# Seven loads of v on ScalarE's queue, and three large products of zeros in place of 48 small ones

## The chip, the cores and the metric

The kernel runs on one core of a Trainium2 chip. The metric is the device time of one execution in microseconds; less is better. The kernel before takes 585.13 us (median of 3 runs, 584.51 to 585.97).

## What is computed

Three stages follow one another. Block retention (a linear attention with decay) over `q`, `k`, `v` of shape (2, 8, 768, 64) in float32, in blocks of 64 positions:

```python
for b in range(nb):
    intra = np.einsum('bhic,bhjc->bhij', qb, kb) * Dmask[None]
    intra = np.einsum('bhij,bhjd->bhid', intra, vb)
    inter = np.einsum('bhid,bhde->bhie', qb * lam_pow[None], kv_state)
    out[:, :, sl] = intra + inter
    kv_state = lam_block[None, :, None, None] * kv_state + np.einsum('bhsd,bhse->bhde', kb * rev_pow[None], vb)
```

Its output, as 1536 rows of 512, goes through two feed-forward stages with hidden width 2048: `h = x @ w_in`, a pointwise function (mish in the first, elu in the second), `g @ w_out`. The weights come as 64-bit floats and are turned into pairs of 32-bit parts on the core.

## The kernel before

Retention goes in chunks of 128 positions: `chunks` has twelve, numbered from 0, the two batches in turn; a chunk holds all 8 heads. The loop `for n in range(NC + 2)` (L368 to L393) is a software pipeline written out by hand. In turn n it issues the loads of k and q of chunk n+3 and of v of chunk n+1 (L369, L370), then weights (`LOAD`, L371), then does: the late part of chunk n-2's output (`second_part`: `xl`, `sd`), scores and decay of chunk n (`sc`, `am`), the transposes of chunk n+1 (`Tp` in PSUM, copied to `T` by ScalarE, L237), `scaled_q` of chunk n+1 (tile `q`), `block_state` (`sbd`, ScalarE, L350), the output products of chunk n-1 (`o`, L305, and the state product `st`, L314) and their copy `xh` (ScalarE, L325). GpSimd makes `kd` and scales `sd`. All these steps are pinned: each engine takes its own in program order.

All loads but the small one of `lam` stand in SyncE's (SP) queue, so the order of their issue is that of L369 to L371 over the turns. Every load of k, q or v brings 256 KB in runs of 256 B (64 floats); tiles `kn`, `qn`, `vn` have four buffers each, so v of chunk n+1 takes the buffer of chunk n-3. A block of weights (`raw`) brings 512 KB, for `w_in` in runs of 1 KB. Weights of the first group are loaded at turns 5 and 8 to 13, and VectorE turns them into pairs beside the chunks (`w_steps`, L86; `STEPS`, L548). After the last scores come two units of the first feed-forward product (`EARLY`), then the rest of it on TensorE.

Before the loop, TensorE is given products of zeros (`idle`): `warm(7)` (seven calls of 128 x 128 by 128 x 128 in float32, two instructions each), then the transposes of chunk 0 in two parts with `warm(2)` between them, then `warm_tiles(24)`: 24 calls with 64 x 64 operands in the four quarters of the array, 48 instructions. `warm(2)` stands once more in turn 0. Nothing reads the results.

Of the kernel before, what the change touches and what calls it, by code (L numbers as in the profile page):

```python
# [8 lines left out]
F32 = mybir.dt.float32  # L9
# [9 lines left out]
def kernel(  # L19
# [12 lines left out]
    nc = tc.nc  # L32
    P = 128
    B, H, S, D = q.shape
# [3 lines left out]
    PR = H // 2  # L38
# [87 lines left out]
    def retention(beside_load, beside_step, at_end):  # L126
# [6 lines left out]
        psO = es.enter_context(tc.tile_pool(name="psO", bufs=1, space=PSUM))  # L133

        chunks = [(b, c) for c in range(NCH) for b in range(B)]
        NC = len(chunks)
        nat, tr, sc, am, q2s, kds, done = {}, {}, {}, {}, {}, {}, {}

        def pin(ins):
            tc.keep_in_program_order(ins)  # L140
            return ins

        def load(n, names, parts=1):
            if not 0 <= n < NC:
                return
            b, c = chunks[n]
            for nm in names:
                nat[n, nm] = io.tile([P, H, D], F32, tag=nm + "n", name=nm + "n")
            for y in range(parts):
                for nm in names:  # L150
                    src, t = {"k": k, "q": q, "v": v}[nm], nat[n, nm]
                    hs = slice(y * H // parts, (y + 1) * H // parts)
                    pin(nc.sync.dma_start(  # L153
                        out=t[:, hs],
                        in_=src[b, hs, c * P:(c + 1) * P, :].rearrange("h p d -> p h d"),
                    ))
# [3 lines left out]
        nc.scalar.dma_start(out=lam_b.rearrange("p h o -> p (h o)"), in_=lam.partition_broadcast(P))  # L160
        load(1, "kq")
        load(2, "kq")
        load(0, "v")

        idle = cst.tile([P, P], F32, name="idle")
# [46 lines left out]
        def warm(count):  # L212
            ps = psO.tile([P, PR, P], F32, tag="o", name="warm")
            for _ in range(count):
                pin(nc.tensor.matmul(ps[:, 0], lhsT=idle, rhs=idle, start=True, stop=True))

        def transposes(n, parts=1):

            T2 = P // 2
            both = wk.tile([P, 2, PR, P], F32, tag="T", name="T")  # L220
            ps = psT.tile([P, 2, 2, PR, T2], F32, tag="T", name="Tp")
            for y in range(parts):
                if y > 0:
                    warm(2)
                rs = slice(y * PR // parts, (y + 1) * PR // parts)
                for z, nm in enumerate(("k", "q")):
                    x = nat[n, nm]
                    for r in range(rs.start, rs.stop):
                        for h in range(2):
                            rows = slice(h * T2, (h + 1) * T2)  # L230
                            pin(nc.tensor.transpose(  # L231
                                ps[:, h, z, r],
                                x[rows, 2 * r:2 * r + 2].rearrange("p h d -> p (h d)"),
                                ident[rows, rows],
                            ))
                if parts == 1:
                    pin(nc.scalar.activation(  # L237
                        out=both.rearrange("p z r (h t) -> p h (z r) t", h=2),
                        in_=ps.rearrange("p h z r t -> p h (z r) t"), func=AF.Copy,
                    ))  # L240
                else:
                    for z in range(2):
                        pin(nc.scalar.activation(
                            out=both[:, z, rs].rearrange("p r (h t) -> p h r t", h=2),
                            in_=ps[:, :, z, rs], func=AF.Copy,
                        ))
            tr[n] = both[:, 0], both[:, 1], ps

        def scaled_k(n):
            if n >= NC:  # L250
                return
            kd = None
            if chunks[n][1] < NCH - 1:
                kd = wk.tile([P, H, D], F32, tag="kd", name="kd", bufs=3)
                pin(nc.gpsimd.tensor_tensor(
                    out=kd, in0=nat[n, "k"], in1=dm[:, :, P - 1:P].to_broadcast([P, H, D]), op=ALU.mult
                ))
            kds[n] = kd

        def scaled_q(n):  # L260
            if n < NC and chunks[n][1] > 0:
                q2 = wk.tile([P, PR, P], F32, tag="q2", name="q2", bufs=3)
                pin(nc.vector.tensor_tensor(  # L263
                    out=q2.rearrange("p r (h t) -> p h r t", h=2), in0=tr[n][2][:, :, 1],
                    in1=lq.rearrange("p r (h t) -> p h r t", h=2), op=ALU.mult,
                ))
                q2s[n] = q2

        def scores(n):
            kT, qT, _ = tr[n]  # L270
            ps = psS.tile([P, 2, PR, P], F32, tag="sc", name="sc")
            for r in range(PR):
                for hh in range(2):
                    rows = slice(hh * D, (hh + 1) * D)
                    last = pin(nc.tensor.matmul(  # L275
                        ps[:, hh, r], lhsT=kT[rows, r], rhs=qT[rows, r], start=True, stop=True
                    ))
            sc[n] = ps
            return last

        def decay(n):
            a = wk.tile([P, 2, PR, P], F32, tag="am", name="am")
            pin(nc.vector.tensor_tensor(
                out=a, in0=sc.pop(n), in1=dm.rearrange("p (r t) i -> p t r i", t=2), op=ALU.mult
            ))
            am[n] = a
# [34 lines left out]
        def first_part(n):  # L321
            o, st = done[n]
            b, c = chunks[n]
            t, col = divmod(n * P, TB)
            pin(nc.scalar.activation(out=xh[t][:, :, col:col + P], in_=o, func=AF.Copy))  # L325
            if st is not None and c > 0:
                pin(nc.gpsimd.tensor_tensor(out=sd[b], in0=sd[b], in1=lc, op=ALU.mult))

        def second_part(n):
            o, st = done[n]  # L330
            b, c = chunks[n]
            t, col = divmod(n * P, TB)
            pin(nc.vector.tensor_tensor(  # L333
                out=xl[t][:, :, col:col + P],
                in0=o,
                in1=xh[t][:, :, col:col + P].bitcast(F32),
                op=ALU.subtract,
            ))
            if st is not None:
                if c > 0:  # L340
                    pin(nc.vector.tensor_tensor(out=sd[b], in0=sd[b], in1=st, op=ALU.add))
                else:
                    pin(nc.vector.tensor_copy(sd[b], st))
# [7 lines left out]
                        out=sbd[b][rows, :, rows], in_=sd[b][rows], func=AF.Copy  # L351
                    ))


        def warm_tiles(count):

            ps = [psO.tile([P, PR, x], F32, tag=t, name="warm") for t, x in (("o", P), ("st", D))]
            for x in range(count):
                y, z = divmod(x % 4, 2)
                rows, cols = slice(y * D, (y + 1) * D), slice(z * D, (z + 1) * D)  # L360
                pin(nc.tensor.matmul(
                    ps[y][cols, 0, 0:D], lhsT=idle[rows, 0:D], rhs=idle[rows, 0:D], start=True, stop=True
                ))

        warm(7)
        transposes(0, 2)
        warm_tiles(24)
        for n in range(NC + 2):  # L368
            load(n + 3, "kq")  # L369
            load(n + 1, "v")  # L370
            beside_load(n, pin)  # L371
            if n >= 2:
                second_part(n - 2)
                beside_step(n, 0, pin)
            if n < NC:
                last = scores(n)
                decay(n)
            if n == 1:
                powers(8, P)
            if n + 1 < NC:  # L380
                transposes(n + 1)
            if n == 0:
                warm(2)
                scaled_k(0)
            if n + 1 < NC:
                scaled_q(n + 1)
            if n >= 2:
                block_state(n - 2)
            if 0 < n <= NC:
                outputs(n - 1)  # L390
                first_part(n - 1)
            scaled_k(n + 1)
            beside_step(n, 1, pin)  # L393
        with tc.issue_after(last.ins):
# [161 lines left out]
    def beside_load(n, pin):  # L556
        for m in LOAD.get(n, ()):
            pin(w_load(m))

    def beside_step(n, place, pin):  # L560
        for _ in range(STEPS.get((n, place), 0)):
            pin(next(todo))
# [6 lines left out]
    def first_units():  # L569
        for _ in todo:  # L570
            pass
        for u in range(EARLY):
            unit(u)
            weights_at(u)

    retention(beside_load, beside_step, first_units)
    open_late()
    for u in range(EARLY):
# [36 lines left out]
```

## Time and profile before

| | us |
|---|---|
| median of 3 runs | 585.13 (584.51 to 585.97) |
| the profiled execution | 584.7 |
| span of its instructions | 582.4 |
| PE busy | 574.4 (99%) |
| DVE busy | 430.9 (74%) |
| ACT busy | 231.5 (40%) |
| POOL busy | 18.9 (3%) |

PE is TensorE, PEld its weight loads, DVE VectorE, ACT ScalarE, POOL GpSimd; SPq is SyncE's queue. The span runs from the first to the last instruction of the program; the time of the execution has 2.3 us more around it. Busy time is an average over stages: retention takes about the first 60 us, the two feed-forward stages the rest.

### The profile page before, as it was taken

To read this page: it belongs to the slowest core of one execution; us is meant where nothing else is said; L and a number is where in the kernel's file an instruction comes from. 1 tells how busy PE (TensorE), PEld (TensorE's weight loads), DVE (VectorE), ACT (ScalarE), POOL (GpSimd) and SP (SyncE) were. 2 spreads that over 40 slices of the span, in tenths; PEclk is the share of its full clock that TensorE was granted. 3 is DMA by queue.
4 is the path that set the end of the run, shared out by engine and by line. 5 is a ranking of instruction groups with operands and counts; after the bars stand their busy time and mean duration, and the time that the engine had idled before them with its cause. 6 is when DMAs were issued, how large, how long until landed. Compare 5 with 4: busy or idle time off the path is not lost.

```text
span 582.4 us, 8221 instructions
## 1 busy us (share of the span) xinstructions
PE 574.4 (99%) x3282; PEld 481.2 (83%) x3282; DVE 430.9 (74%) x798; ACT 231.5 (40%) x390; POOL 18.9 (3%) x28
## 2 busy tenths in 40 slices
PE   7999999999999999999999999999999999999997
PEld 6988888888888888888888888888888888888886
DVE  5769999998399726993599956995499957944342
ACT  3655554344134124233346445555145235235220
POOL 4430000000000000000000000000000000000000
PEclk9999999999999999999999999999999999999999
DMA  9998333334023301322022221321022310000112
GB/s 172 214 219 233 109 110 108 110 111 142 0 74 108 109 1 37 106 79 69 1 72 73 73 73 36 110 74 71 1 73 72 109 36 1 1 1 0 73 54 92
DMA packets 61030, 46.67 MB, mean 80 GB/s; under 512 B 38848, under 2 KB 55488, under 8 KB 60992
## 3 DMA queue, kind: packets, MB, share of 16 engines
q1 hardware_dynamic: 60848, 46.14, 28.2%
q8 instruction: 26, 0.43, 0.3%
q14 instruction: 12, 0.10, 0.1%
q10 hardware_dynamic: 144, 0.00, 0.0%
HBM read 43.00 MB, written 3.15 MB: 79 GB/s over the span
## 4 chain that ended last, share of the span: by engine, by line
PE 93%; DMA 2%; DVE 2%; SPq 1%; ACT 1%; issue 1%; ACTq 0%
PE h L423 44%; PE y L465 43%; PE o L305 2%; PE y L480 2%; DMA qn<-in_q_dram 1%; DMA vn<-in_v_dram 1%; SPq L153 1%; PE sc L275 1%; PE Tp L231 1%; PE st L314 0%; DVE xl L333 0%; DVE b L104 0%; DVE u L111 0%; DVE q L263 0%; ACT xh L325 0%
## 5 line engine op out<-in xcount | busy, mean ns | idle before, releaser
L423 PE MATMUL h<-xh,w 128*128 128x512 f32 x768 | 240.7, 389 | 0.1
L423 PEld LDWEIGHTS h<-xh,w 128*128 128x128 f32 x768 | 144.1, 188 | 30.5 <-ACT w L118 0.6
L423 PE MATMUL h<-xl,w 128*128 128x512 f32 x384 | 149.4, 389 | 0.0
L465 PE MATMUL y<-w,g 128*128 128x512 f32 (+1 forms) x588 | 132.5, 385 | 0.0
L465 PEld LDWEIGHTS y<-w,g 128*128 128x128 f32 x588 | 108.9, 188 | 22.1
L465 PE MATMUL y<-g,w 128*128 128x512 f32 x528 | 121.5, 389 | 0.0
L465 PEld LDWEIGHTS y<-g,w 128*128 128x128 f32 x528 | 99.1, 188 | 20.6
L493 DVE TENSOR_TENSOR acc<-acc,y 128x512 f32<-128x512 f32 (+1 forms) x73 | 49.4, 677 | 58.6 <-PE y L465 58.6
L433 DVE TENSOR_TENSOR g<-g,g 128x512 fp32r<-128x512 f32 x96 | 65.9, 687 | 30.0 <-ACT g L432 27.5
L423 PEld LDWEIGHTS h<-xl,w 128*128 128x128 f32 x384 | 72.1, 188 | 14.9
L118 ACT ACTIVATE w<-m 128x512 fp32r<-128x512 f32 x64 | 40.2, 628 | 102.0 <-PE h L423 55.2
L432 ACT ACTIVATE g<-g 128x512 fp32r<-128x512 f32 x96 | 60.2, 628 | 16.3 <-DVE g L450 14.8
L119 DVE TENSOR_TENSOR w<-m,w 128x512 fp32r<-128x512 f32 x64 | 43.9, 686 | 24.4 <-ACT w L118 23.7
L441 ACT ACTIVATE g<-h 128x512 f32<-128x512 f32 x48 | 28.5, 596 | 71.1 <-PE h L423 71.1
L447 ACT ACTIVATE e<-h 128x512 f32<-128x512 f32 x48 | 28.6, 596 | 59.0 <-PE h L423 58.0
L450 DVE SCALAR_TENSOR_TENSOR g<-e,h 128x512 f32<-128x512 f32 x48 | 32.8, 683 | 17.1 <-ACT e L448 17.0
L104 DVE SCALAR_TENSOR_TENSOR b<-raw,b 128x512 int32<-128x512 int32 x64 | 44.1, 690 | 0.4
L111 DVE SCALAR_TENSOR_TENSOR u<-raw,u 128x512 f32<-128x512 uint32 x64 | 43.7, 684 | 0.2
L116 DVE TENSOR_TENSOR m<-b,u 128x512 f32<-128x512 f32 x64 | 43.7, 684 | 0.1
L448 ACT ACTIVATE e<-e 128x512 f32<-128x512 f32 x48 | 30.3, 631 | 1.1
L98 DVE TENSOR_SCALAR m<-m 128x512 f32<-128x512 f32 x64 | 27.1, 424 | 0.1
L107 DVE TENSOR_SCALAR u<-b 128x512 int32<-128x512 int32 x64 | 26.8, 420 | 0.4
(52 smaller groups left out, 304.3 us busy)
## 6 DMA issues: line engine op xcount, KB each, us to landing
raw<-in_moe_w_in_dram SPq DMA_DIRECT2D x32, 512.0 KB, 3.7
raw<-in_moe_w_out_dram SPq DMA_DIRECT2D x32, 512.0 KB, 3.3
vn<-in_v_dram SPq DMA_DIRECT2D x12, 256.0 KB, 5.2
kn<-in_k_dram SPq DMA_DIRECT2D x11, 256.0 KB, 5.2
qn<-in_q_dram SPq DMA_DIRECT2D x11, 256.0 KB, 5.0
out_dram<-acc SPq DMA_DIRECT2D x11, 256.0 KB, 2.0
kn<-in_k_dram SPq DMA_DIRECT2D x2, 128.0 KB, 3.5
qn<-in_q_dram SPq DMA_DIRECT2D x2, 128.0 KB, 3.6
```

The lines of the kernel that those rows point to most:

```text
L104: yield nc.vector.scalar_tensor_tensor(out=b, in0=hw, scalar=-0x40000000, in1=b, op0=ALU.bitwise_and, op1=ALU.bitwise_or)
L111: yield nc.vector.scalar_tensor_tensor(out=uf, in0=lw, scalar=2.0 ** -52, in1=uf, op0=ALU.mult, op1=ALU.mult)
L116: yield nc.vector.tensor_tensor(out=mf, in0=bf, in1=uf, op=ALU.add)
L118: nc.scalar.activation(out=w[:, 0], in_=mf, func=AF.Copy)
L119: yield nc.vector.tensor_tensor(out=w[:, 1], in0=mf, in1=w[:, 0].bitcast(F32), op=ALU.subtract)
L423: nc.tensor.matmul(h, lhsT=lt, rhs=rt, start=(kk == 0 and n == 0), stop=(kk == KD - 1 and n == 2),)
L432: nc.scalar.activation(out=gg[:, 0], in_=g, func=AF.Copy)
L433: nc.vector.tensor_tensor(out=gg[:, 1], in0=g, in1=gg[:, 0].bitcast(F32), op=ALU.subtract)
L448: nc.scalar.activation(out=e, in_=e, func=AF.Exp, scale=-1.0)
L450: nc.vector.scalar_tensor_tensor(out=g, in0=e, scalar=-1.0, in1=h, op0=ALU.add, op1=ALU.max)
L465: nc.tensor.matmul(y, lhsT=lt, rhs=rt, start=(i == 0 and n == 0), stop=(i == G - 1 and n == 2),)
L493: nc.vector.tensor_tensor(out=dst, in0=dst, in1=y, op=ALU.add)
```

## The change

Two edits. First, `load` takes the queue that issues as a parameter. For n below `OTHER` = 4 the load of v of chunk n+1 stays where it was; from n = 4 on, that is for chunks 5 to 11 (the sixth and later, seven loads), it is issued by ScalarE, in program order behind `first_part(n - 1)`, whose instruction on ScalarE is `xh` of chunk n-1 (the first part of x). On ScalarE the next pinned instruction behind it is the copy `T` of the next turn. Second, `warm_tiles` goes, and `warm(3)` stands in place of `warm_tiles(24)`: three calls with full 128 x 128 operands, writing tile `o` only.

```diff
+        OTHER = 4
-        def load(n, names, parts=1):
+        def load(n, names, parts=1, queue=nc.sync):
...
-                    pin(nc.sync.dma_start(
+                    pin(queue.dma_start(
...
-        def warm_tiles(count):
-
-            ps = [psO.tile([P, PR, x], F32, tag=t, name="warm") for t, x in (("o", P), ("st", D))]
-            for x in range(count):
-                y, z = divmod(x % 4, 2)
-                rows, cols = slice(y * D, (y + 1) * D), slice(z * D, (z + 1) * D)
-                pin(nc.tensor.matmul(
-                    ps[y][cols, 0, 0:D], lhsT=idle[rows, 0:D], rhs=idle[rows, 0:D], start=True, stop=True
-                ))
-
         warm(7)
         transposes(0, 2)
-        warm_tiles(24)
+        warm(3)
         for n in range(NC + 2):
             load(n + 3, "kq")
-            load(n + 1, "v")
+            if n < OTHER:
+                load(n + 1, "v")
...
             if 0 < n <= NC:
                 outputs(n - 1)
                 first_part(n - 1)
+            if n >= OTHER:
+                load(n + 1, "v", queue=nc.scalar)
             scaled_k(n + 1)
```

## Rows read from the trace of the kernel before

**Rows 1.** Page, the span in 40 slices: busy tenths of PE, granted TensorE clock.

```profile
PE   7999999999999999999999999999999999999997
PEclk9999999999999999999999999999999999999999
```

**Rows 2.** Chain of waits in order of time: start us, us, what.

```profile
6.75 6.17 DMA vn<-in_v_dram
...
33.52 6.58 DMA qn<-in_q_dram
...
61.93 24.77 PE h L423 x108
```

**Rows 3.** Busy time in windows: the first line names the columns.

```profile
core 0: us, PE busy (x) PEld busy (x) DVE busy (x) ACT busy (x) POOL busy (x), PEclk, DMA share, GB/s
28.00:32.00 4.00, 4.00 (x86) 3.86 (x84) 2.90 (x5) 2.50 (x5) 1.64 (x2) 1.00 1.15 233
...
35.00:36.00 1.00, 1.00 (x26) 0.93 (x24) 1.00 (x2) 0.47 (x1) 0.18 (x1) 1.00 1.08 353
...
56.00:60.00 4.00, 4.00 (x22) 3.04 (x22) 4.00 (x11) 0.67 (x2) 0.00 (x0) 1.00 0.05 19
```

**Rows 4.** Timeline, 29.5 to 36.3 us: start, us, engine, line, tiles [idle before <-releaser].

```profile
29.54 0.60 ACT L325 ACTIVATE xh<-o 128x512 fp32r<-128x512 f32 x1
...
31.56 1.02 ACT L237 ACTIVATE T<-Tp 128x1024 f32<-128x1024 f32 x1 [1.42 <-PE Tp L231]
...
33.49 0.60 ACT L325 ACTIVATE xh<-o 128x512 fp32r<-128x512 f32 x1
...
34.12 0.69 DVE L333 TENSOR_TENSOR xl<-o,xh 128x512 fp32r<-128x512 f32 x1 [0.81 <-ACT xh L325]
...
35.05 1.22 DVE L283 TENSOR_TENSOR am<-sc,dm 128x1024 f32<-128x1024 f32 x1
...
36.28 1.04 PE L305 MATMUL o<-am,vn 128*64 128x128 f32 x16
```

**Rows 5.** Timeline, TensorE at chunk 9's transposes and at chunk 10's output.

```profile
40.14 0.47 PE L231 MATMUL Tp<-ident,qn 64*128 64x64 f32 x8 [1.02 <-DMA qn<-in_q_dram]
...
53.11 1.04 PE L305 MATMUL o<-am,vn 128*64 128x128 f32 x16
```

**Rows 6.** Timeline, issues in SyncE's queue, 33 to 48 us.

```profile
33.52 0.89 SPq L153 DMA_DIRECT2D qn<-in_q_dram  x1
34.50 2.33 SPq L153 DMA_DIRECT2D vn<-in_v_dram  x1
...
46.13 0.47 SPq L153 DMA_DIRECT2D vn<-in_v_dram  x1
46.65 1.08 SPq L75 DMA_DIRECT2D raw<-in_moe_w_in_dram  x1
```

**Rows 7.** Time to landing: all loads of v; on the page, loads of 128 KB.

```profile
DMA to landing us min/median/max: 4.4/5.2/8.0
...
kn<-in_k_dram SPq DMA_DIRECT2D x2, 128.0 KB, 3.5
```

**Rows 8.** Timeline, 5 to 14 us: the products of zeros and what follows them.

```profile
5.08 0.52 PEld L215 LDWEIGHTS warm<-idle 128*128 128x128 f32 x4
5.08 0.71 PE L215 MATMUL warm<-idle 128*128 128x128 f32 x4
...
6.30 0.93 PE L361 MATMUL warm<-idle 64*64 64x64 f32 x48
...
6.41 0.66 ACT L243 ACTIVATE T<-Tp 128x256 f32<-128x256 f32 x2 [0.56 <-PE Tp L231]
...
13.06 1.09 PE L305 MATMUL o<-am,vn 128*64 128x128 f32 x16 [1.46 <-DMA vn<-in_v_dram]
```

**Rows 9.** Instructions and their fetches: page, then transfers in 9.5:10 and 36.6:37 us.

```profile
PE 574.4 (99%) x3282; PEld 481.2 (83%) x3282; DVE 430.9 (74%) x798; ACT 231.5 (40%) x390; POOL 18.9 (3%) x28
...
q8 instruction: 26, 0.43, 0.3%
...
q8 instruction: 1, 0.02, 16.4%
...
q8 instruction: 1, 0.02, 19.8%
```

## The prediction

> **What bounds the kernel now.** I read the page's slices first. TensorE (PE) is 90% busy or more in all slices but the first and the last, at granted clock 0.9 to 1.0 throughout [rows 1]; so the time can change only where PE is not yet full. The chain of waits says where that ends: it goes through v of chunk 0 (6.75 to 12.92 us), later through q of chunk 9 (33.52 to 40.10 us), and from 61.93 us on PE runs without a gap to the last store [rows 2]. All of the change lies ahead of 61.93 us; what follows is a fixed 520.5 us (582.4 less 61.93). The sum is therefore: by how much does the point at 61.93 us move?
>
> Three limits lie close together there. **Loads:** while chunks stream, the DMA engines move 233 GB/s; a 256 KB load of k, q or v costs 262,144 B / 233 GB/s = 1.13 us, three per chunk 3.4 us. Weights, in longer packets, go at 353 GB/s, 524,288 B / 353 = 1.49 us each [rows 3]. **PE:** one chunk costs 3.95 us (`xh` of chunk 4 starts at 29.54, of chunk 5 at 33.49 us) [rows 4], and the one place where it stops late in the stage is 1.02 us for q of chunk 9 [rows 5]. **VectorE (DVE):** busy 4.00 of 4 us from 56 to 60 us, where before it was busy 2.90 [rows 3]: late in the stage the weight steps fill it, so a delay met there goes to the end in full.
>
> **Removed from SP, added to ScalarE (ACT).** Seven loads, v of chunks 5 to 11, leave SP's queue. On SP, k and q of the following chunks and the weights move up by one place for each v. The sequencer time that this frees (0.47 to 2.33 us per issue [rows 6]) buys nothing by itself: the loads move at the data rate [rows 3], and SP is ahead of them by the 5.2 us from issue to landing [rows 7]. I count 0 for it; the bytes to be moved before 61.93 us are the same.
>
> On ACT each issue stands behind `xh` of chunk n-1. ACT is then idle until the transposes are copied: 1.42 us between `xh` (ends 30.14) and `T` at 31.56 us [rows 4], and since a sequencer can go on to an issue while its engine works, the 0.60 us of `xh` may cover it too: 2.02 us at best, 1.42 at worst. Behind the issue are queued `T`, the two `sbd` copies and the next `xh`; for `xh` waits DVE (`xl` 0.81 us idle for it), behind that `am`, which ends at 36.27 us, and PE wants it at 36.28 [rows 4]. So this chain has no slack: what an issue takes beyond its cover is lost one to one. The trace has no 256 KB issue on ACT; the bounds are SP's shortest and longest, 0.47 and 2.33 us [rows 6]. ACT's queue has no backlog of its own, so I take the short one: 0 us, with 7 x (2.33 - 2.02) = 2.2 us as the upper bound. The slot's last readers are the products of chunk n-3, two turns of the loop earlier, so the added wait for them ends before it is reached: 0.
>
> **Order of landing.** This is the main term. Now SP issues in the order in which PE needs the data: k, then q of chunk 9 at 33.52 us, then v of chunk 7 at 34.50 us [rows 6]. Afterwards ACT issues v of chunk 7 as soon as `xh` of chunk 5 is under way (33.49 us [rows 4]), on a queue without the 5 us of backlog that SP's loads show (median 5.2 us to landing [rows 7]). PE wants that v in `outputs(7)`, after the transposes of chunk 9, whose q is already late [rows 5]. If the DMA engines serve both queues in turn, some of v's 1.13 us falls ahead of q. Bounds: 0 (SP's backlog goes first) and +1.13. q still has most of its 6.58 us [rows 2] before it when v starts, so I take nearly all, +1.0 us.
>
> The Trainium skill (DMA: Bandwidth & Descriptors, Queues, rings and completion order) says that an engine takes its queues in turn, packet by packet. No run here has yet shown two loaded queues; by that rule the term is +1.0, and by strict order of issue it is 0.
>
> **Three large products for 48 small ones.** On PE 48 small ones take 0.93 us from 6.30 us; four large ones take 0.71 us at a pace of 0.52/4 = 0.13, so six (three calls are six instructions, as 7 calls are 14) take 0.71 + 2 x 0.13 = 0.97 us [rows 8]. PE waits at their end for `T`, which ends at 7.07 us, either way, and at 13.06 us it still waits 1.46 us for v of chunk 0 [rows 8]: 0 us, cover 1.46 us. I take the granted clock to stay: the large products keep at least as much of the array busy. Were PE at 1.2 GHz afterwards, a chunk's 3.95 us of PE work would double, of which the stop hides 1.46: bound 0 to +2.5, taken 0.
>
> It has a side effect. PE gets 42 products and 42 weight loads fewer. The page counts 26 instruction fetches, 0.43 MB [rows 9], for 2 x 3282 PE instructions: 65 B each, a fetch of 16 KB per 252. With 84 fewer, each fetch comes a third of a period later, 84/170 of a chunk's instructions (86 and 84 in 4 us [rows 3]), some 2 us. Two fetches stand at 9.5 to 10 and 36.6 to 37 us [rows 9], right before the two loads that land late: v of chunk 0 takes 6.17 and q of chunk 9 6.58 us [rows 2] against the median of 5.2 [rows 7], 1.0 and 1.4 us more. Moved to about 38.7 us, the later fetch comes too late to hold up q. Bounds 0 and -1.4; I take -0.8, since the fetch may hold up k and q of chunk 10 instead. The 1.0 us at chunk 0 brings PE ahead, but q of chunk 9 is the later limit: 0 there.
>
> **The last v's.** SP, without v, issues the weights of the first group earlier, in one backlog, while v of chunk 10, until now issued at 46.13 us ahead of weights (46.65 us [rows 6]), comes from ACT behind `xh` of chunk 8, some 46.6 us. With a turn each, 1,024 packets of v meet 1,024 packets of weights (two loads of 512 packets): 1.13 + 2 x 1.49 = 4.1 us. A load of 128 KB with nothing ahead lands in 3.5 us, 2.9 without its data [rows 7]: 46.6 + 2.9 + 4.1 = 53.6 us, and PE wants it at 53.11 [rows 5]. Bounds 0 and +1.1 (a delay carried over); taken +0.4. The weights that come earlier gain nothing, since DVE is busy with older work.
>
> **Sum:** 0 + 0 + 1.0 - 0.8 + 0 + 0.4 = +0.6 us. The profiled execution took 584.7 us (span 582.4, 2.3 around it), so it would be 585.3; the median of the runs shown is 585.13, 0.4 above, and I forecast 585.7 us.
>
> **Rivals.**
> Faster: v does not get ahead of q, because SP's backlog is served first, and the moved fetch takes the whole 1.02 us stop away [rows 5]; with PE also ahead by what it gains at chunk 0, at most 1.0 + 1.0. For: loads, PE and DVE are within 0.5 us per chunk, so a small relief counts. Against: the bytes are the same, so a v that gives way to q is itself late. Time: 585.1 - 1.0 = 584.1, at most 583.1. Chance 0.22.
>
> Slower: ACT is held at its issue. If ACT's issue has to wait until the one that SP is at is through, it takes: up to 2.33 + 0.47 - 2.02 = 0.8 us each time, for PE through `T`, `xh`, `xl`, `am` [rows 4]. It decides from the point where wait and issue together pass 2.02 us. Three of seven issues that meet one of SP's as long as the 2.33 us [rows 6] cost 2.4, with the sum +3.0: 588.1 us. Against it: SP has fewer issues left to meet. Chance 0.20.
>
> The Trainium skill (Perfetto Trace Analysis, DMA Instruction — HWDGE (DVE, Sync)) tells of one descriptor block that an issuer locks; no row here shows such a wait.
>
> Nothing happens: v lands early, q at the same time, 585.1 us. Chance 0.13. My forecast: 0.45.
>
> **How the numbers follow.** A difference of under 0.3% (1.76 us) can't be told from none. Beyond it on the slow side lie most of the held ACT (0.16) and the upper end of my own case, chunks 9 and 10 both late (0.06): 0.22. On the fast side only the end of the faster rival: 0.06. The rest, 0.72, is within. The range goes from 583.9 (stop gone, a little more) to 588.3 (held ACT).
>
> **What would show it.** Right: q of chunk 9 lands at 40 to 41 us, the v's from ACT land in under 5 us, the later fetch stands near 38.7 us, DVE is full from chunk 9 on, and gap-free PE starts at 62 to 63 us. Wrong: no stop at chunk 9 (rival faster); `DMA_DIRECT2D` on ACT over 1.4 us with `T` idle for it (rival slower); a granted clock below 1 in the first 15 us, which would upset the term of the products.

## The result, and the profile after

The changed kernel takes **589.42 us** (median of 7 runs, 588.43 to 590.22) beside 585.79 us of the kernel before (7 runs, 584.09 to 587.59): ratio 1.0065, 95% interval 1.0049 to 1.0081. It is slower by 0.65%, some 3.8 us. The forecast was 585.7 us, within 0.3% of no change, with a range up to 588.3: it was wrong.

The profiled execution has a span of 586.7 us (before 582.4). The first view to read is again the chain of waits of the changed kernel (start us, us, what).

```profile
10.18 6.07 DMA vn<-in_v_dram
...
33.65 6.39 DMA kn<-in_k_dram
...
66.19 24.78 PE h L416 x108
```

The point from which PE runs without a gap lies at 66.19 us, before at 61.93 [rows 2]: +4.26 us, and the span is longer by 4.3. So the whole loss lies ahead of that point, as the prediction had assumed; but the late link of the chain is now a load of k (issued at 33.65, landed at 33.65 + 6.39 = 40.04 us) where it was q of chunk 9. Where PE met it is in the timeline of the changed kernel (start, us, engine, line, tiles, idle before and its releaser). First ScalarE, at the place of [rows 4]:

```profile
32.99 1.02 ACT L238 ACTIVATE T<-Tp 128x1024 f32<-128x1024 f32 x1 [2.85 <-DMA kn<-in_k_dram]
34.04 0.85 ACT L351 ACTIVATE sbd<-sd 64x256 f32<-64x256 f32 x2
34.92 0.60 ACT L326 ACTIVATE xh<-o 128x512 fp32r<-128x512 f32 x1
40.12 0.37 ACTq L154 DMA_DIRECT2D vn<-in_v_dram  x1
40.59 1.02 ACT L238 ACTIVATE T<-Tp 128x1024 f32<-128x1024 f32 x1 [5.07 <-DMA kn<-in_k_dram]
41.08 0.37 ACTq L154 DMA_DIRECT2D vn<-in_v_dram  x1
```

and TensorE behind it:

```profile
38.86 0.64 PE L315 MATMUL st<-vn,kd 128*64 128x64 f32 x16
41.67 1.82 PE L276 MATMUL sc<-T 64*128 64x128 f32 x16 [2.18 <-ACT T L238]
...
47.16 1.16 PE L276 MATMUL sc<-T 64*128 64x128 f32 x16
```

Before, `T` of chunk 8, the scores of chunk 8 and those of chunk 9 were:

```profile
35.53 1.03 ACT L237 ACTIVATE T<-Tp 128x1024 f32<-128x1024 f32 x1 [1.45 <-PE Tp L231]
...
37.72 1.16 PE L275 MATMUL sc<-T 64*128 64x128 f32 x16
...
42.90 1.16 PE L275 MATMUL sc<-T 64*128 64x128 f32 x16
```

Read them together. `xh` of chunk 5 ends at 35.52 us; the next thing in ScalarE's queue is the issue of v of chunk 7. It takes 0.37 us, but it begins only at 40.12 us, and `T` of chunk 8, queued behind it, begins at 40.59 us, where before it began at 35.53: +5.06 us. `T` had about 1.1 us to spare there, so the scores of chunk 8 begin at 41.67 instead of 37.72 us, +3.95, and from the scores of chunk 9 on (47.16 instead of 42.90) everything is late by the 4.26 us. One wait costs nearly all of it. The view of waits (30 to 62 us: who waited, for whom, us in total, times, longest) counts it together with the 2.85 us of `T` of chunk 7, which put the next scores back by only 0.30 us:

```profile
ACT T L238 <- DMA kn<-in_k_dram: 7.9, 2, 5.1
```

The odd thing is the releaser. `T` copies transposes that PE had finished long before; v of chunk 7 goes into a buffer that has nothing to do with k. Yet the issue starts 0.08 us after **k of chunk 10** has landed. The trace does not say why; the order of each engine's instructions as the builder (the library that turns the kernel's calls into instructions) wrote it, with the semaphores (counters by which one waits for another) for which each waits, does. The 29th of SP is the load of k of chunk 10, the 33rd of ScalarE that of v of chunk 7:

```
29 L154 DMA kn_639<-in_k_dram 128x8x64 [waits DMAHW6_49,PE_49,Pool_49]
33 L154 DMA vn_635<-in_v_dram 128x8x64 [waits DMAHW6_49,DMAHW2_49]
```

Each load of SyncE's and ScalarE's queues reports its end on one of eight semaphores, DMAHW0 to DMAHW7, which the builder hands out in turn, in its own order of all instructions; and a load waits until the one before it on the same semaphore has landed, whatever buffers the two use. While all loads were on SP, the one eight places back had landed some 4 us before (v of chunk 7 was issued at 34.50 us, q of chunk 7, the one before it on its semaphore, had landed at 30.30). In the changed kernel the builder's order lets SP run far ahead of ScalarE: k and q of chunk 10 stand ahead of v of chunk 7, so v gets the semaphore of a load issued shortly before it, and ScalarE, with all its work behind, stands until that one has landed. Its issues on either side stand as close behind theirs: v of chunk 6 goes out at 32.52 us (k of chunk 8 landed at 32.49), v of chunk 8 at 41.08 (q of chunk 10 landed at 41.01). This is the theory tested below: **the wait for the semaphore's previous load.**

### The profile page after: what moved, and what is told of

The parts are those of the page before. It is cut to its first block, busy times and chain, and to the rows that moved or that the text cites. A ratio compares the mean times of both kernels' runs of the same rounds, so it can differ in the third digit from the quotient of the medians.

```text
span 586.7 us, 8133 instructions
## 1 busy us (share of the span) xinstructions
PE 576.1 (98%) x3240; PEld 482.6 (82%) x3240; DVE 431.1 (73%) x798; ACT 231.5 (39%) x390; POOL 18.8 (3%) x28
## 4 chain that ended last, share of the span: by engine, by line
PE 92%; DMA 3%; DVE 2%; SPq 2%; ACT 0%; issue 0%; ACTq 0%
PE h L416 44%; PE y L458 43%; PE o L306 2%; PE y L473 2%; SPq L154 2%; PE sc L276 1%; DMA kn<-in_k_dram 1%; DMA vn<-in_v_dram 1%; DMA raw<-in_moe_w_out_dram 1%; PE Tp L232 1%; PE st L315 0%; ACT T L238 0%; DVE u L111 0%; DVE b L104 0%; DVE q L264 0%
## 5 line engine op out<-in xcount | busy, mean ns | idle before, releaser
L118 ACT ACTIVATE w<-m 128x512 fp32r<-128x512 f32 x64 | 40.2, 628 | 102.1 <-PE h L416 55.2
```

The costliest lines, as they stand in the source:

```text
L118: nc.scalar.activation(out=w[:, 0], in_=mf, func=AF.Copy)
```

## The experiments

Its rivals: the order of landing (v takes the DMA engines' time from k and q), the products, and the granted clock (it fell in the changed kernel after the stop). ScalarE held during its issue is out already, by the 0.37 us above.

### Each half of the change alone

The kernel before with only the products changed:

```
-        warm_tiles(24)
+        warm(3)
```

> The three large products alone; all loads stay in SP's queue. All theories: they are not where the time went. v of chunk 0 lands 1 us earlier because the instruction fetch at 9.7 us moves to about 12 us, q of chunk 9 is held up 0 to 0.7 us less, the granted clock stays at 2.4 GHz from 4.4 us on. Expected ratio to the kernel before 0.998 to 1.001 (-1.0 to +0.5 us). Were the products the cause, it would be +3 to +4 us.

Measured 584.34 us (11 runs), ratio 0.9986 (0.9973 to 1.0). The kernel before with only v moved, the 48 small products kept:

```
+            if n < OTHER:                       # OTHER = 4
                 load(n + 1, "v")
...
+            if n >= OTHER:
+                load(n + 1, "v", queue=nc.scalar)
```

> The seven loads of v on ScalarE alone, with the 48 small products kept. All three theories of the loss (wait on a shared completion semaphore; order of landing; ACT held at its issue) put it here: +3 to +5 us against before. The semaphore theory says where: ScalarE's issue for v of chunk 7 starts within 0.1 us of the landing of k of chunk 10, some 5 us after its turn, with the copy T of chunk 8 right behind it. The order theory says: the wait shows on PE for q of chunk 9.

Measured 590.21 us (4 runs), ratio 1.009 (1.0074 to 1.0106). Its view of waits, 30 to 62 us:

```profile
ACT T L238 <- DMA kn<-in_k_dram: 5.4, 1, 5.4
```

and the busy times of the stretch with the loss (columns as in [rows 3]):

```profile
39.00:45.00 6.00, 3.37 (x72) 3.09 (x68) 2.29 (x4) 3.75 (x6) 1.64 (x2) 1.00 1.11 245
```

The loss is in the move of v, with the same wait (v of chunk 7 goes out at 40.37 us, k of chunk 10 landed at 40.29), and it is there at a granted clock of 1.0: the products cost nothing, and the clock is not needed for it. Gap-free PE starts at 67.31 us, 1.1 later than in the changed kernel; here PE also stops 1.11 us for v of chunk 7, which lands at 46.31.

### Only one v moved

```
-            if n < OTHER:
+            if n != 6:
                 load(n + 1, "v")
...
-            if n >= OTHER:
+            if n == 6:
                 load(n + 1, "v", queue=nc.scalar)
```

> Of the seven loads only v of chunk 7 on ScalarE; its completion semaphore was last used by k of chunk 8, which lands at 33 to 34 us, when xh of chunk 5 runs. Semaphore theory: no wait over 0.5 us, so no loss: 583.5 to 585.5 us (the three large products are in). Order theory: v of chunk 7 goes ahead of q of chunk 9, which lands up to 1.1 us later; PE's stop for it grows from 1.0 to 2 us: 585.5 to 587 us.

Measured 584.70 us (10 runs), ratio 1.0003 (0.9988 to 1.0017): nothing lost. The same v is on the same queue at the same place; what differs is the number of loads ahead of it in the builder's order, so that its semaphore was last used by k of chunk 8, landed at 31.87 us. ScalarE's timeline of this kernel:

```profile
33.35 0.39 ACTq L154 DMA_DIRECT2D vn<-in_v_dram  x1
33.37 0.60 ACT L326 ACTIVATE xh<-o 128x512 fp32r<-128x512 f32 x1
35.39 1.02 ACT L238 ACTIVATE T<-Tp 128x1024 f32<-128x1024 f32 x1 [1.42 <-PE Tp L232]
```

The issue goes out while `xh` runs, and `T` starts as before, after the 1.42 us of [rows 4]. This is what the prediction had described; here it is true.

### The wait alone, with loads of no size

To take bytes and the order of landing out of it: the kernel before, every load where it was, and at the place of v of chunk 7 on ScalarE's queue one, or four, loads of 4 KB into spare tiles that nothing reads.

```
+            for x in range(1 if n == 6 else 0):          # e14_tiny4: 4 for 1
+                pin(nc.scalar.dma_start(out=spare[x], in_=lam.partition_broadcast(P)))
             scaled_k(n + 1)
```

> The kernel before with every load where it was, plus one load of 4 KB (lam, 32 B to each partition, into a spare tile that nothing reads) on ScalarE's queue at the place where the changed kernel issues v of chunk 7, behind xh of chunk 5. In the builder's order its completion semaphore was last used by k of chunk 9, which landed at 38.26 us in the kernel before. Semaphore theory: the small load waits for that landing, T of chunk 8 behind it starts at 38.3 us instead of 35.53 (+2.8); as the changed kernel turned +5.06 us at T of chunk 8 into +4.26 at the end, some 0.8 us is absorbed: +2.0 us, 586.3 to 587.3 us. Theory of the bytes, the order of landing or two queues sharing the DMA engines: 4 KB is nothing, one issue of 0.4 us is covered by the 1.42 us for which ScalarE is idle there: 584.4 to 585.2 us, T of chunk 8 at 35.5.

> The same with four such loads of 4 KB at that one place. In the builder's order their semaphores were last used by k of chunk 9, q of chunk 9, k of chunk 10 and v of chunk 8, which landed at 38.26, 40.10, 42.26 and 44.84 us in the kernel before. Semaphore theory: the last of the four holds T of chunk 8 until 44.9 us (+9.4 against 35.53), so the end moves by some 8.6 us: 592.5 to 594.5 us. Theory of the bytes, the order of landing or two queues: 16 KB takes 0.07 us at 233 GB/s and four issues 1.5 us of ScalarE's 1.42 to 2.02 us: 584.4 to 585.5 us.

One load: 586.41 us (10 runs), ratio 1.0027 (1.0012 to 1.0042). Four: 593.94 us (4 runs), ratio 1.0157 (1.0142 to 1.0173). Both forecasts are met, at +1.6 and +9.2 us for 4 and 16 KB. With one, the chain's k of chunk 9 and ScalarE's timeline:

```profile
32.81 5.14 DMA kn<-in_k_dram
```

```profile
37.97 0.34 ACTq L394 DMA_DIRECT2D spare<-in_lam_dram  x1
38.41 1.02 ACT L238 ACTIVATE T<-Tp 128x1024 f32<-128x1024 f32 x1 [4.40 <-DMA kn<-in_k_dram]
```

32.81 + 5.14 = 37.95 us, and the issue goes out at 37.97. With four, the chain has v of chunk 8, and ScalarE's timeline the last of the four issues:

```profile
38.86 5.16 DMA vn<-in_v_dram
```

```profile
44.05 0.33 ACTq L394 DMA_DIRECT2D spare<-in_lam_dram  x1
44.48 1.02 ACT L238 ACTIVATE T<-Tp 128x1024 f32<-128x1024 f32 x1 [10.73 <-DMA spare<-in_lam_dram]
```

v of chunk 8 lands at 44.02 us; the fourth issue goes out at 44.05, and the three others at 37.65, 39.16 and 41.33, each 0.02 or 0.03 us after the load on its semaphore has landed (37.62, 39.14 and 41.31 us). Each issue takes 0.33 or 0.34 us. Gap-free PE starts at 63.32 us with one load and at 71.02 with four. The rivals gave 584.4 to 585.5 us for both. So the wait costs this much by itself, without bytes; that it is what the changed kernel pays is read from its issue, 0.08 us behind the landing, and from the kernel with one v, where wait and loss are both absent.

### Two attempts to move the wait away

First, the turn of the semaphores shifted by two, with two loads of 4 KB in SP's queue:

```
             beside_load(n, pin)
+            for _ in range(2 if n == 10 else 0):
+                pin(nc.sync.dma_start(out=spare[_], in_=lam.partition_broadcast(P)))
```

> The changed kernel and two loads of 4 KB (lam into spare tiles, which nothing reads) in SP's queue behind the weights of turn 10. Loads take one of eight completion semaphores in turn, so with two loads more v of chunk 7 gets the one of v of chunk 6 in place of the one of k of chunk 10. Semaphore theory: its issue starts at about 37.9 us (landing of v of chunk 6) in place of 40.1, T of chunk 8 follows at once, PE's stop of 2.2 us there goes, the granted clock does not fall, and the time is 2 to 4 us below the changed kernel: 585.5 to 587.5 us. Order theory and held issue: nothing that they speak of changes, 589 to 590 us.

Measured 593.01 us (4 runs), ratio 1.0138 (1.0124 to 1.0152). ScalarE's timeline:

```profile
38.42 0.37 ACTq L154 DMA_DIRECT2D vn<-in_v_dram  x1
...
44.68 0.37 ACTq L154 DMA_DIRECT2D vn<-in_v_dram  x1
45.16 1.02 ACT L239 ACTIVATE T<-Tp 128x1024 f32<-128x1024 f32 x1 [3.73 <-DMA kn<-in_k_dram]
```

v of chunk 7 goes out at 38.42 us instead of 40.12, as forecast, after v of chunk 6 landed at 38.40. But the shift gives v of chunk 8 the semaphore of k of chunk 11, and `T` of chunk 9 now waits 3.73 us; v of chunk 8 then lands beside the weights and PE waits 2.5 us for it. The place of the wait came out as the theory says, the time did not: I had followed one load and not the six behind it.

Second, fewer buffers (three for k and q in place of four; v keeps four), so that SP's loads stand less far ahead of ScalarE's in the builder's order:

```
-                nat[n, nm] = io.tile([P, H, D], F32, tag=nm + "n", name=nm + "n")
+                nat[n, nm] = io.tile([P, H, D], F32, tag=nm + "n", name=nm + "n", bufs=4 if nm == "v" else 3)
```

> The changed kernel with three buffers each for k and q in place of four (v keeps four). SP can then run one chunk less ahead in the builder's order, and the loads of v get completion semaphores whose last load landed earlier: v of chunk 7 that of q of chunk 8 (about 33 us), v of chunk 8 that of k of chunk 10 (about 40 us) where the changed kernel had k and q of chunk 10. Semaphore theory: v of chunk 7 is issued by 35 us, T of chunk 8 does not wait for it, and at most some 1 us of waiting is left, at chunk 8; 585 to 587.5 us. Order theory: the loads land in the same turn as in the changed kernel, 588 to 590 us.

Measured 588.33 us (4 runs), ratio 1.005 (1.003 to 1.007). v of chunk 7 goes out at 34.48 us without a wait, and `T` of chunk 8 at 36.52. The next one is caught:

```profile
41.56 0.37 ACTq L154 DMA_DIRECT2D vn<-in_v_dram  x1
42.03 1.02 ACT L238 ACTIVATE T<-Tp 128x1024 f32<-128x1024 f32 x1 [2.98 <-DMA kn<-in_k_dram]
```

Again k of chunk 10 (landed at 41.48 us), now ahead of v of chunk 8. The time is in the range that was written for the order of landing (588 to 590 us) and not in that of the semaphore (585 to 587.5), and PE's stops say why:

```profile
43.11 1.16 PE L276 MATMUL sc<-T 64*128 64x128 f32 x16 [0.38 <-ACT T L238]
45.58 1.09 PE L306 MATMUL o<-q,sbd 128*64 128x128 f32 x16 [0.81 <-DVE xl L334]
53.02 1.09 PE L306 MATMUL o<-am,vn 128*64 128x128 f32 x16 [2.40 <-DMA vn<-in_v_dram]
```

The wait at `T` of chunk 9 reaches PE as 0.38 us, and 0.81 through `xl`; the largest stop, 2.40 us, is for v of chunk 9, which goes out at 42.82 us among the blocks of weights and lands 10.15 us later. So with the long wait gone, the late landing is a second cost of the move. Some 1 us is there ahead of both: `T` of chunk 7 starts at 32.58 us (before 31.56) with no load in its way, and the 16 scores at 8.44 us took 2.08 us in this execution where they take 1.16 in the changed kernel; whether the buffers did that is not shown.

### The clock, and GpSimd's queue

Large products of zeros in the stop at chunk 8 of the changed kernel, to keep PE busy there:

```
+            for _ in range(8 if n == 8 else 0):
+                pin(nc.tensor.matmul(ps[:, 0, 0], lhsT=idle, rhs=idle, start=True, stop=True))
```

> The changed kernel with eight large products of zeros (sixteen instructions, about 2.1 us) on TensorE ahead of the scores of chunk 8, written to the scores' own bank before they start; they run while PE waits for T of chunk 8. If the fall of the granted clock to 1.2 GHz after that stop has its own price (16 scores 1.82 in place of 1.16 us, the other products of the chunk alike), 1.2 to 1.6 us come back: 587.8 to 588.3 us. If the clock costs nothing, because loads or VectorE would have ended last anyway, 589 to 590 us.

Measured 589.88 us (4 runs), ratio 1.0082 (1.0061 to 1.0104): no gain over the changed kernel, although in the profiled execution the granted clock now stays at 1.0 from 39 to 62 us. The fall has no price of its own in the end time, and this trace shows what takes its place: PE stops 0.58 us for `xl` and 0.70 us for v of chunk 7, which lands at 46.72 us, so that from the scores of chunk 8 to those of chunk 9 it is 5.52 us (42.73 to 48.25), beside 5.49 in the changed kernel (41.67 to 47.16).

The seven v's from GpSimd's queue (in two halves of 4 heads each):

```
-                load(n + 1, "v", queue=nc.scalar)
+                load(n + 1, "v", 2, queue=nc.gpsimd)
```

> The changed kernel with the seven loads issued by GpSimd in place of ScalarE, at the same place of the loop, each in two halves (its queue takes fewer pieces at a time). GpSimd's loads have completion semaphores of their own and ScalarE issues nothing. Semaphore theory: T is never held up, 584 to 587 us, unless GpSimd's issue takes so long that kd comes late. Order theory: two queues still take turns, 586 to 590 us, with PE waiting for k or q.

Measured 603.25 us (4 runs), ratio 1.0302 (1.0285 to 1.0319). The semaphore theory had forecast 584 to 587 us; it is much the worst. Its view of waits, 20 to 75 us:

```profile
POOL vn L154 <- issue: 16.5, 8, 4.9
...
PE o L306 <- DMA vn<-in_v_dram: 11.8, 5, 4.6
...
POOL vn L154 <- DMA qn<-in_q_dram: 5.6, 2, 3.4
...
POOL vn L154 <- DMA kn<-in_k_dram: 4.9, 1, 4.9
```

`T` waits for no load any more, as forecast. But GpSimd stands idle ahead of its issues, 16.5 us of it for nothing that the profile shows ("issue"); where the view names k and q, the program gives the issue no semaphore of theirs. What each of the thirteen issues behind the first does follow is the landing of the half load before it in GpSimd's own queue, by 0.30 or 0.31 us: of the two halves of v of chunk 6, the first,

```profile
31.45 0.79 POOL L154 DMA_DIRECT2D vn<-in_v_dram  x1 [2.25 <-DMA qn<-in_q_dram]
37.14 0.75 POOL L154 DMA_DIRECT2D vn<-in_v_dram  x1 [4.91 <-DMA kn<-in_k_dram]
```

lands at 36.83 us, and the second goes out at 37.14. In this run GpSimd's queue thus has one half under way at a time; why is not shown. GpSimd's own work (`kd`, for which SP's next k waits, and `sd`) is queued behind, the v's go out late (the last half at 74.28 us), and PE waits 11.8 us for them. So GpSimd, too, is held by the issues among its work, and this test of the semaphores brought in a longer wait of another kind.

### The stop at chunk 9, and a combination

The kernel before, with the first block of weights loaded one turn of the loop later, so that k and q of chunk 9 go ahead of it:

```
-    LOAD = {5: (0,), 8: (1,), 9: (2,), 10: (3,), 11: (4,), 12: (5,), 13: (6, 7)}
+    LOAD = {6: (0,), 8: (1,), 9: (2,), 10: (3,), 11: (4,), 12: (5,), 13: (6, 7)}
```

> The kernel before with the first block of weights loaded in turn 6 in place of 5, behind q of chunk 9 and v of chunk 7. It measures what the stop of 1.02 us at chunk 9 is worth: those loads land 1.5 to 2 us earlier, the stop goes, the weights land at about 41 us, when VectorE wants them. If the way from there to the gap-free part is one to one, 583.6 to 584.3 us; if VectorE has slack after all, or now waits for the weights, 584.5 to 585.5 us.

Measured 584.25 us (11 runs), ratio 0.9984 (0.9974 to 0.9994). q of chunk 9 lands at 37.55 us, the 1.02 us stop of [rows 5] is gone, and gap-free PE starts at 61.48 us. So that stop was on the path, but only 0.45 us of its 1.02 reached this point in the trace, where the prediction let such a delay go "to the end in full". With the products changed as well:

> The kernel before with three large products of zeros for the 48 small ones and the first block of weights loaded one turn of the loop later; all of v stays on SyncE's queue. If the two small gains add (0.4 and 0.5 us against the kernel before): 583.4 to 584.2 us. If both act on the same stop at chunk 9, the second adds nothing: 584.2 to 584.7 us.

Measured 584.44 us (11 runs), ratio 0.999 (0.9981 to 0.9999): the gains don't add up to anything that is told apart from one of them alone. The profiled execution of the two together has its gap-free point at 60.79 us, 1.1 earlier than before; the median of the runs doesn't confirm that much.

## Why the prediction was wrong

**The step that failed** is the sentence on the added wait: "The slot's last readers are the products of chunk n-3, two turns of the loop earlier, so the added wait for them ends before it is reached: 0." The part on the readers is true; it left out that an issue waits for more than its buffer. v of chunk 7, whose turn had come by the end of `xh` at 35.52 us, waited 4.6 us more for the previous load on its semaphore and went out 0.08 us behind its landing; the gap-free point moved by +4.26 us where the term said 0. The issue itself was rightly taken as short: 0.37 us against the cover of 1.42.

**The chain behind it** (`T`, `sbd`, `xh`, `xl`, `am`, PE) was named rightly, and "lost one to one" nearly so: +5.06 us at `T` became +4.26 at the end. But `T` of a later chunk has some 1.1 us to spare against the scores that need it, so small delays are taken up: v of chunk 6 put `T` of chunk 7 back by 1.43 us (32.99 after 31.56), and PE's next scores by 0.30 (34.07 after 33.77).

**The slower rival** had the right place, direction and almost the time (588.1 us) with a wrong cause. It put the delay into issues that collide; no ScalarE issue took more than 0.39 us, while those of SP took 0.98 to 2.20 from 33 to 41 us, and the one at 40.12 us ran its 0.37 us while SP was at an issue of its own (39.77 to 41.45 us). The Trainium skill (Perfetto Trace Analysis, DMA Instruction — HWDGE (DVE, Sync)) tells of a descriptor block that an issuer locks; no run here shows a wait for it.

**The order of landing** (+1.0 us) was right in kind and too large. In the kernel with one v moved, ScalarE's v is issued 0.28 us behind SP's q of chunk 9 and lands first. The issue-to-landing time of that v, then that of q:

```profile
DMA to landing us min/median/max: 6.1/6.1/6.1
...
DMA to landing us min/median/max: 7.1/7.1/7.1
```

33.35 + 6.1 = 39.5 us against 33.07 + 7.1 = 40.2. Beside the kernel with the products alone, which differs in that one load, q of chunk 9 is late by 0.5 us (39.65 there) and gap-free PE by 0.33 (61.99 after 61.66): by these two traces the term is some 0.3 to 0.5 us. The Trainium skill's rule that an engine takes its queues in turn (DMA: Bandwidth & Descriptors, Queues, rings and completion order) agrees with v landing first. In the changed kernel itself the term did not arise: q of chunk 9 landed at 38.94 us, before v of chunk 7 was issued.

**The products** came out at 0 on PE: six large ones take 0.94 us (forecast 0.97) where the small ones took 0.93 [rows 8]:

```profile
6.04 0.94 PE L216 MATMUL warm<-idle 128*128 128x128 f32 x6
```

The granted clock stays at 1.0 up to the stop at chunk 8, so the bound of +2.5 us was not needed. **The moved fetch** was right in its direction: the one at 36.6 to 37 us [rows 9] comes at 37.82 us with the products alone and at 39.68 in the changed kernel (forecast 38.7). Its worth was forecast as 0.8 us and is less: with the products alone q of chunk 9 lands 0.45 us earlier (39.65 after 40.10) and gap-free PE starts 0.27 us earlier. The time, 0.9986 with an interval that ends at 1.0, says no more, and that the fetch is what moved q is not tested apart from the products.

**SP's relief**, taken as 0, wasn't neutral. Without v in its queue SP runs further ahead, in the builder's order and on the chip (k of chunk 10 issued at 33.65 us, before at 36.94), and this is what put a recent load on v's semaphore. **The last v's** (+0.4 us) cost nothing: v of chunk 10 is issued at 50.77 us, landed in 3.0, and PE stops for none of them.

## What to carry to other kernels

Before a load is moved to another engine's queue, list every wait that its issue will carry, in the order as the builder wrote it: the buffer's, and that of the completion semaphore, which the load takes over from another load; on an engine that computes, everything queued behind the issue pays for it. The length of such a wait is the landing of the previous load on that semaphore less the time at which the issue is reached; what the engine behind has to spare comes off it (some 1.1 us here), and it changes when a load is added or removed anywhere ahead in the order. To test a suspected wait, put a load of a few KB at the same place: it carries the wait and nothing else.

## What the runs showed that was not expected

**The granted clock fell after a stop, and in this kernel it cost nothing in the end.** In the profiled execution of the changed kernel PE stood for 2.18 us ahead of 41.67 us; from 42.0 to 45.4 us the granted clock was 0.5, the lower of the two levels (1.2 GHz), and 16 products of scores took 1.82 us instead of the 1.16 of those at 51.11 us. Before the fall, at it and behind it:

```profile
41.00:42.00 1.00, 0.33 (x5) 0.33 (x6) 0.35 (x1) 0.98 (x2) 0.00 (x0) 0.99 0.80 176
42.00:45.40 3.40, 3.40 (x43) 3.28 (x41) 2.50 (x4) 2.03 (x4) 1.65 (x2) 0.50 1.14 284
45.40:46.00 0.60, 0.60 (x14) 0.60 (x14) 0.50 (x1) 0.55 (x3) 0.00 (x0) 1.00 1.12 272
```

In the kernel with v alone PE stood for 2.06 us at the same place without a fall, and it was no faster. Of the seven executions of the changed kernel, four have a mean granted clock of 0.997, as the profiled one has with its 3.4 us, and three of 1.0: their medians are 589.14 and 589.42 us. What decides whether it falls is not shown.

**A v on ScalarE's queue lands in 3 to 10 us, by what is in SP's queue.** In the changed kernel v of chunk 7 took 4.9 us and v of chunk 8, issued 0.96 us later, 7.0 (beside three blocks of weights); v of chunk 10, with little beside it, 3.0. In the kernel with v alone, v of chunk 8 is the chain's longest load:

```profile
41.37 9.44 DMA vn<-in_v_dram
```

So a v that goes out late meets the weights as well: in the kernel with two small loads and in that with fewer buffers PE waited 2.5 and 2.4 us for such a one.
